# A long matmul pipeline on one core: transfers issued later, transposes on another queue, chunks entering one by one, another order of the last visits

## The chip, the cores and the metric

One core of a Trainium2 chip. The metric is the device time of one execution in microseconds (us), and lower is better. A run is marked slow when it is over 1.5% above the fastest run of the same kernel; only fast runs are compared unless the text says otherwise. PE is TensorE, DVE VectorE, ACT ScalarE, POOL GpSimd, SP SyncE. SP, ACT and POOL also issue DMAs, each from a queue of its own, in program order. A crossbar transpose is a DMA that transposes while it copies.

## The reference

A short causal convolution over the sequence, then a mixing layer with two 4224 x 4224 matrices:

```python
# x: (8, 4224, 192), weight: (8 heads, 7 taps)
w = softmax(weight)                                   # per head
out[b, s, h, g] = sum_k w[h, k] * x_pad[b, s + k, h, g]      # conv; its result is called x below
theta = x @ w_theta
zr, zi = x * cos(theta), x * sin(theta)
y = einsum('ts,bsd->btd', w_tok_r, zr) + einsum('ts,bsd->btd', w_tok_i, zi)
u = x + y
return u + maximum(u @ w_ch, 0)
```

The two big products are nearly all of the work. All inputs and the output are float32; the products run in bfloat16.

## The kernel before

The 4224 tokens are 33 chunks of 128 rows (source side) and 17 units of 256 rows (target side; the last has 128). A chunk is prepared once: conv on PE, copy out by ACT, transpose, theta on PE, sine and cosine on ACT, products and differences on DVE. It then stays in SBUF while 17 visits use it. A visit takes one unit and up to 11 resident chunks, multiplies, and adds the result to four partial sums of 128 x 768 float32, which live in DRAM between visits. A unit of 256 rows takes 7 products (of two halves each) per chunk instead of 8, so 14 matmuls of 384 columns.

```python
SLOTS = 11
FIRST = (0, 0, 1, 1, 2, 3, 3, 4, 5, 6, 7)      # visit in which each of the first chunks enters
# ... (cut)
    def conv(self, hp):
        ...
        if hp == H // 2 - 1:                       # the conv of the chunk is complete
            for a in range(NQ):                    # kept in DRAM as the residual of the end
                nc.sync.dma_start(out=xs[t0 : t0 + Q, :], in_=...)
# ... (cut)
    def transposed(u, by_pe, uT=None):
        if not by_pe:                              # from chunk 11 on, and for all outputs
            nc.sync.dma_start_transpose(out=uT[:, :, :], in_=u)
            return uT
# ... (cut)
class Visit:
    def load(self, q, tag):                        # one of six buffers for partial sums
        ...
        nc.sync.dma_start(out=d, in_=part[self.u][q][:, :])
        if self.final:                             # the last visit of a unit: add the residual
            nc.sync.dma_start(out=xr, in_=xs[self.rows(q), self.cols(q)])
            nc.gpsimd.tensor_tensor(out=d, in0=d, in1=xr, op=ALU.add)

    def add(self, q, y, g, begins=False, ends=False):
        ...                                        # DVE: d += y
        if self.final:
            self.output(q)                         # cast, transpose, u @ w_ch, relu, store
            return
        nc.sync.dma_start(out=part[self.u][q][:, :], in_=self.d[q])
        free_sums(self.tag[q])                     # issues the load of the next sum at once
```

The order of every engine is fixed when the program is built: a list of events (load, conv, transpose, theta, weights) is placed against the PE time that the program expects.

## Time and profile before

| | |
|---|---|
| time | 1751.27 us median of 4 runs (1741.36 to 1756.26) |
| span of the profiled run | 1748.8 us |
| PE busy / DVE / ACT / POOL | 85% / 61% / 19% / 40% |
| granted PE clock, mean | 0.92 |
| products of a visit of 11 chunks, undisturbed | 25.0 us |

"Busy in chosen stretches" has one row per stretch: its length, then for each engine the busy time and the number of instructions, the granted PE clock (1.00 is full), the busy share of the DMA engines (it can exceed 1) and the bytes moved in GB/s. A line of the waits says who waited, for whom, and the total, the number and the longest of the waits. The lines themselves are in the prediction.

### The profile page before, as it was taken

The numbers are of one execution on the slowest core, as the hardware profiler recorded it, in microseconds if no ns is written. First come the engines' busy times: TensorE is split into PE (matmuls) and PEld (weight loads), VectorE is DVE, ScalarE is ACT, GpSimd is POOL, SyncE is SP. The second block draws the span as 40 slices with busy tenths as digits, with TensorE's granted clock in tenths as the row PEclk, the third lists the DMA queues.
The fourth block names the chain that finished last, engine by engine and source line by source line (L and its number), as shares of the span: only waits on it lengthen the run. The fifth ranks groups of instructions, "written<-read, shape, count | busy, mean of one in ns | idle before, by whom it ended". The sixth has DMA issues, their size and how long they took to land. (4 is left out here: it accounts for less than half of the span.)

```text
span 1748.8 us, 25577 instructions
## 1 busy us (share of the span) xinstructions
PE 1487.3 (85%) x9390; PEld 904.5 (52%) x9390; DVE 1068.7 (61%) x1830; ACT 339.1 (19%) x582; POOL 703.2 (40%) x1176
## 2 busy tenths in 40 slices
PE   5779999999887878699999889899888878887543
PEld 3445666665554545466665555555555545554322
DVE  5778544543676767576657667668656636576533
ACT  4444212112221212110012112121111100111111
POOL 6654433332433334323333423423544435456621
PEclk7689999999998989899999999999999988998865
DMA  7898766665999999977889998999889868899865
GB/s 108 135 180 162 145 122 121 126 120 129 182 187 187 197 204 209 190 169 185 187 203 179 188 187 185 182 188 186 177 187 184 181 155 172 179 220 224 176 160 143
DMA packets 366861, 301.66 MB, mean 172 GB/s; under 512 B 174864, under 2 KB 316432, under 8 KB 366736
## 3 DMA queue, kind: packets, MB, share of 16 engines
q1 hardware_dynamic: 192464, 215.18, 44.5%
q0 software_dynamic: 174272, 84.86, 42.6%
q8 instruction: 73, 1.20, 0.3%
q14 instruction: 52, 0.43, 0.1%
HBM read 250.21 MB, written 106.56 MB: 204 GB/s over the span
## 5 line engine op out<-in xcount | busy, mean ns | idle before, releaser
L390 PEld LDWEIGHTS <-w 128*128 128x128 bf16 x6600 | 654.8, 100 | 467.6 <-issue 68.9
L313 POOL DMA_DIRECT2D st<-in_moe_w_tok_i_dram x476 | 257.0, 548 | 478.7 <-DVE w L333 428.6
L313 POOL DMA_DIRECT2D st<-in_moe_w_tok_r_dram x476 | 256.2, 546 | 284.6 <-DVE w L333 266.7
L405 DVE TENSOR_TENSOR d<-y,d 128x384 f32<-128x384 f32 x290 | 158.2, 552 | 238.0 <-PE y L390 188.0
L333 DVE STREAM_TRANSPOSE w<-st 128x768 bf16<-128x768 bf16 (+5 forms) x333 | 258.8, 813 | 60.6 <-PE x L390 59.8
L390 PE MATMUL x<-zi,w 128*128 128x384 bf16 x1122 | 218.9, 350 | 0.0
L390 PE MATMUL x<-zr,w 128*128 128x384 bf16 x1122 | 203.5, 332 | 0.0
L390 PE MATMUL s<-zt,w 128*128 128x384 bf16 x1056 | 188.4, 331 | 14.9 <-DVE d L405 14.9
L390 PE MATMUL y<-zr,w 128*128 128x384 bf16 x1056 | 189.8, 331 | 13.1 <-DVE d L405 13.1
L390 PE MATMUL y<-zt,wl 128*128 128x384 bf16 x1056 | 195.4, 339 | 5.5 <-DVE d L405 5.5
L390 PE MATMUL y<-zt,w 128*128 128x384 bf16 x1122 | 197.3, 329 | 1.5 <-ACT y L423 1.4
L287 PEld LDWEIGHTS <-uT 128*128 128x128 bf16 x792 | 82.1, 114 | 215.9 <-DMA uT<-xz 96.0
L377 POOL TENSOR_TENSOR d<-d,xr 128x768 f32<-128x768 f32 x66 | 109.7, 1663 | 193.8 <-DMA d<-part 157.8
L390 PE MATMUL s<-zi,w 128*128 128x384 bf16 x1056 | 185.8, 330 | 0.0
L287 PE MATMUL v<-wth,uT 128*128 128x192 bf16 x528 | 70.8, 287 | 105.6 <-DMA uT<-xz 87.8
L390 PEld LDWEIGHTS <-wl 128*128 128x128 bf16 x1056 | 105.9, 101 | 79.4 <-issue 15.9
L217 DVE TENSOR_SCALAR ang<-v 128x384 f32<-128x384 f32 x132 | 69.0, 551 | 122.7 <-PE v L287 120.1
L229 ACT ACTIVATE zr<-ang,half_pi 128x768 bf16<-128x768 f32 x66 | 60.6, 932 | 427.2 <-DVE ang L217 244.9
L348 DVE TENSOR_TENSOR w<-w 128x1408 bf16<-128x1408 bf16 (+10 forms) x174 | 134.2, 771 | 4.9 <-PE s L390 4.7
L405 DVE TENSOR_TENSOR d<-x,d 128x384 f32<-128x384 f32 x92 | 50.5, 554 | 120.3 <-PE x L390 78.5
L477 DVE SCALAR_TENSOR_TENSOR d<-v,d 128x384 f32<-128x384 f32 x132 | 68.0, 549 | 74.3 <-PE v L287 74.0
L405 DVE TENSOR_TENSOR d<-s,d 128x384 f32<-128x384 f32 x200 | 104.7, 536 | 14.2 <-PE s L390 10.5
(64 smaller groups left out, 876.4 us busy)
## 6 DMA issues: line engine op xcount, KB each, us to landing
part<-d SPq DMA_DIRECT2D x172, 384.0 KB, 3.7
d<-part SPq DMA_DIRECT2D x172, 384.0 KB, 4.3
out_dram<-d SPq DMA_DIRECT2D x66, 384.0 KB, 3.9
st<-in_moe_w_tok_r_dram POOLq DMA_DIRECT2D x260, 88.0 KB, 4.8
st<-in_moe_w_tok_i_dram POOLq DMA_DIRECT2D x260, 88.0 KB, 4.3
xs<-xz SPq DMA_DIRECT2D x132, 96.0 KB, 4.8
xr<-xs SPq DMA_DIRECT2D x66, 192.0 KB, 2.9
xw<-in_x_dram POOLq DMA_DIRECT2D x129, 96.0 KB, 5.4
```

The lines of the kernel that those rows point to most:

```text
L217: dve(nc.vector.tensor_scalar(out=af[:, k * 2 * D : (k + 1) * 2 * D], in0=channel_mix(self.xT[g], k, wth), scalar1=-CLAMP, scalar2=CLAMP, ...
L229: act(nc.scalar.activation(out=z[:, g * HN : (g + 1) * HN], in_=self.ang[g], func=AT.Sin, **({"bias": half_pi[:], "scale": 1.0} if i == 0 ...
L287: pe(nc.tensor.matmul(v[:, b * D : (b + 1) * D], lhsT=tT[:, 3 * k + b + i, :], rhs=w[:, 2 * b + i, :], start=(i == 0), stop=(i == 1),), D)
L313: nc.gpsimd.dma_start(out=st[a * Q : (a + 1) * Q, :, 0 : self.n * Q], in_=w[t * P : (t + 1) * P, t0 : t0 + self.n * Q].rearrange("(bt i) s ...
L333: dve(nc.vector.transpose(w[:, c:ce, :, :], st[:, :, c * Q : ce * Q].rearrange("p bt (c j) -> p c bt j", j=Q),))
L348: dve(nc.vector.tensor_tensor(out=flat(o), in0=flat(self.w[p]), in1=flat(self.w[q]), op=op))
L377: nc.gpsimd.tensor_tensor(out=d, in0=d, in1=xr, op=ALU.add)
L390: pe(nc.tensor.matmul(y[:, 0:PC], lhsT=weights[self.v].block(a, c), rhs=zs[c].operand(b, g), start=(start and c == self.lo), stop=(c == se ...
L405: dve(nc.vector.tensor_tensor(out=o, in0=y[:, 0:PC], in1=o, op=ALU.add))
L477: dve(nc.vector.scalar_tensor_tensor(out=dk, in0=channel_mix(uT, k, wch_[0]), scalar=0.0, in1=dk, op0=ALU.max, op1=ALU.add,))
```

## The change

Four intents: transfers go out only when their data is ready, so that a queue does not stand at them; the crossbar transposes move from SP's to ACT's queue; the first eleven chunks enter one per visit and are prepared within the visits; and the last visits alternate large and small, with four more sum buffers from the space of the chunk loads that have ended.

```diff
-    FIRST = (0, 0, 1, 1, 2, 3, 3, 4, 5, 6, 7)
+    FIRST = tuple(range(SLOTS))
@@ the order of the visits
+    while large:
+        sequence.append(large.pop(0))
+        if small:
+            sequence.append(small.pop())
@@ transposed
-            nc.sync.dma_start_transpose(out=uT[:, :, :], in_=u)
+            nc.scalar.dma_start_transpose(out=uT[:, :, :], in_=u)
@@ conv: the stores of the residual become keep(), called after the second transpose
@@ load of a sum
-                nc.sync.dma_start(out=xr, in_=xs[self.rows(q), self.cols(q)])
+                later(4.0, lambda: self.residual(q))     # issued on POOL, added 3 us later
@@ store of a sum (the store of an output likewise, 1.0 and 6.0)
-            nc.sync.dma_start(out=part[self.u][q][:, :], in_=self.d[q])
-            free_sums(self.tag[q])
+            def store():
+                nc.sync.dma_start(out=part[self.u][q][:, :], in_=self.d[q])
+                later(6.0, lambda: free_sums(self.tag[q]))
+            later(1.5, store)
@@ outputs: three in flight instead of four
@@ after the last conv
+        big = [wk.tile([P, 2, HN], F32, name="late", tag="xw") for _ in range(2)]
+        tags.extend(t[:, k, :] for t in big for k in range(2))
@@ load of a chunk two ahead instead of one
-            (-24.0, lambda: c + 1 < NCH and c + 1 > 2 and load_chunk(c + 1)),
+            (-15.0, lambda: c + 2 < NCH and load_chunk(c + 2)),
@@ early chunks: conv and transposes in visit c-2, theta and the rest in visit c-1
   ... (the rest cut)
```

More of the change, by code (lines that the diff above doesn't have):

```diff
@@ L119 @@
         visits.append((v % UNITS, here[0], here[-1] + 1))
+    settled = enter[-1]
+    large = [v for v in range(settled, len(visits))]
+    small = []
+    while len(large) > len(small) + 3:
+        small.append(large.pop())
+    sequence = list(range(settled))
+    while large:
+        sequence.append(large.pop(0))
+        if small:
+            sequence.append(small.pop())
     seen = [0] * UNITS
@@ L203, in conv, with keep @@
                 self.xf = self.xz[:, :, :].rearrange("p b d -> p (b d)")
-                for a in range(NQ):
-                    t0 = tokens(self.c, a)
-                    nc.sync.dma_start(
-                        out=xs[t0 : t0 + Q, :], in_=self.xf[a * Q : (a + 1) * Q, :]
-                    )
-                self.xT, self.ang = [], []
+                self.xT, self.ang = [], []
+        def keep(self):
+            for a in range(NQ):
+                t0 = tokens(self.c, a)
+                nc.sync.dma_start(
+                    out=xs[t0 : t0 + Q, :], in_=self.xf[a * Q : (a + 1) * Q, :]
+                )
         def transpose(self, g):
@@ L295, in __init__ @@
         def __init__(self, v):
-            self.u, self.lo, self.hi = visits[v]
+            self.u, self.lo, self.hi = visits[sequence[v]]
             self.n = self.hi - self.lo
@@ L364, in __init__ @@
             self.quarters = [3, 1, 0, 2] if self.pair else [1, 0]
-            self.d, self.tag = {}, {}
+            self.d, self.tag, self.missing = {}, {}, set()
         def load(self, q, tag):
-            pool, n = (dpool, 6) if tag == "sums" else (wk, 2)
-            d = pool.tile([P, HN], F32, name="d", tag=tag, bufs=n)
+            d = dpool.tile([P, HN], F32, name="d", tag="d") if tag is None else tag
             self.d[q], self.tag[q] = d, tag
@@ L374, in load, with residual, add @@
             if self.final:
-                xr = wk.tile([P, HN], BF16, name="xr", tag="xz")
-                nc.sync.dma_start(out=xr, in_=xs[self.rows(q), self.cols(q)])
+                self.missing.add(q)
+                later(4.0, lambda: self.residual(q))
+        def residual(self, q):
+            d = self.d[q]
+            xr = wk.tile([P, HN], BF16, name="xr", tag="xz")
+            nc.gpsimd.dma_start(out=xr, in_=xs[self.rows(q), self.cols(q)])
+            def add():
                 nc.gpsimd.tensor_tensor(out=d, in0=d, in1=xr, op=ALU.add)
+                self.missing.remove(q)
+            later(3.0, add)
         def rows(self, q):
@@ L390, in product @@
                 pe(nc.tensor.matmul(
-                    y[:, 0:PC], lhsT=weights[self.v].block(a, c),
+                    y[:, 0:PC], lhsT=self.w.block(a, c),
                     rhs=zs[c].operand(b, g),
@@ L398, in add @@
         def add(self, q, y, g, begins=False, ends=False):
-            while q not in self.d:
-                output_step()
+            while q not in self.d or q in self.missing:
+                if delayed:
+                    delayed.pop(0)[2]()
+                else:
+                    output_step()
             o = self.d[q][:, g * PC : (g + 1) * PC]
@@ L410, in add @@
                 return
-            nc.sync.dma_start(out=part[self.u][q][:, :], in_=self.d[q])
-            free_sums(self.tag[q])
+            def store():
+                nc.sync.dma_start(out=part[self.u][q][:, :], in_=self.d[q])
+                stored.add((self.u, q, self.hi))
+                later(6.0, lambda: free_sums(self.tag[q]))
+            later(1.5, store)
         def items(self):
             gs = range(NG)
+            self.w = weights[sequence.index(self.v)]
             x = [None] * NG
@@ L459, in output @@
         def output(self, q):
-            if len(outputs) == 4:
+            if len(outputs) == 3:
                 output_step()
-            made[0] += 1
-            if made[0] % 2:
-                ub = wk.tile([P, HN], BF16, name="ub", tag="ang")
-                uT = None
-            else:
-                both = wk.tile([P, 2, HN], BF16, name="ubT", tag="xw")
-                ub = both[:, 0, :]
-                uT = both[:, 1, :].rearrange("p (k s) -> p k s", s=P)
+            turn[0] += 1
+            if turn[0] % 3:
+                both = wk.tile([P, 2, HN], BF16, name="ubT", tag="ang")
+                ub, uT = both[:, 0, :], both[:, 1, :]
+            else:
+                ub, uT = (wk.tile([P, HN], BF16, name=n, tag="uT") for n in ("ub", "uT"))
+            uT = uT.rearrange("p (k s) -> p k s", s=P)
             act(nc.scalar.activation(out=ub, in_=self.d[q], func=AT.Copy))
-            outputs.append((clock[0] + 8.0, self, q, transposed(ub, False, uT)))
+            outputs.append((pos[0] + 8.0, self, q, transposed(ub, False, uT)))
         def output_end(self, q, uT):
@@ L481, in output_end, with store, later @@
             bs = slice(q % 2 * B // 2, (q % 2 + 1) * B // 2)
-            nc.sync.dma_start(
-                out=out[bs, self.rows(q), :].rearrange("b s d -> s b d"),
-                in_=d[:, :].rearrange("p (b d) -> p b d", d=D),
-            )
-            free_sums(self.tag[q])
+            def store():
+                nc.sync.dma_start(
+                    out=out[bs, self.rows(q), :].rearrange("b s d -> s b d"),
+                    in_=d[:, :].rearrange("p (b d) -> p b d", d=D),
+                )
+                later(6.0, lambda: free_sums(self.tag[q]))
+            later(1.0, store)
     wch_ = []
     outputs = []
-    made = [0]
-    tags = ["sums"] * 6
-    order = [Visit(v) for v in range(len(visits))]
+    delayed = []
+    stored = set()
+    pos = [0.0]
+    def later(us, fn):
+        delayed.append((pos[0] + us, len(made), fn))
+        made.append(None)
+        delayed.sort(key=lambda x: x[:2])
+    made = []
+    turn = [0]
+    tags = [None] * 6
+    order = [Visit(v) for v in sequence]
     waiting = [(vi, q) for vi in order for q in vi.quarters]
@@ L500, in load_sums @@
         while waiting and tags:
-            vi, q = waiting.pop(0)
+            vi, q = waiting[0]
+            if not (vi.first or (vi.u, q, vi.lo) in stored):
+                return
+            waiting.pop(0)
             vi.load(q, tags.pop(0))
@@ L579 @@
         weights[0].load()
-    load_chunk(2)
     def idle(n, s):
@@ L590, with length, last_conv @@
     cost = PC / 2400 + 0.0025
-    starts, t = [], 0.0
-    for u, lo, hi in visits:
-        starts.append(t)
+    starts, t = {}, 0.0
+    for v in sequence:
+        u, lo, hi = visits[v]
+        starts[v] = t
         t += (hi - lo) * parts(u) * cost
-    starts.append(t)
     events = []
+    def length(v):
+        u, lo, hi = visits[v]
+        return (hi - lo) * parts(u) * cost
+    def last_conv():
+        big = [wk.tile([P, 2, HN], F32, name="late", tag="xw") for _ in range(2)]
+        tags.extend(t[:, k, :] for t in big for k in range(2))
+        load_sums()
     def chunk_events(c, t0, n):
         for at, fn in (
-            (-24.0, lambda: c + 1 < NCH and c + 1 > 2 and load_chunk(c + 1)),
+            (-15.0, lambda: c + 2 < NCH and load_chunk(c + 2)),
             (-18.0, lambda: (chunks[c].conv(0), chunks[c].conv(1))),
-            (-15.0, lambda: (chunks[c].conv(2), chunks[c].conv(3))),
+            (-15.0, lambda: (
+                chunks[c].conv(2), chunks[c].conv(3), c == NCH - 1 and last_conv()
+            )),
             (-14.0, lambda: chunks[c].transpose(0)),
-            (-13.5, lambda: chunks[c].transpose(1)),
+            (-13.5, lambda: (chunks[c].transpose(1), chunks[c].keep())),
             (-5.0, lambda: chunks[c].theta(0)),
@@ L620, in chunk_events, with early, early_events @@
             events.append((t0 + 2 * n * cost + at, fn))
-    def early_events(c, t0):
-        for off, fn in (
-            (0.0, lambda: c + 1 < NCH and c + 1 > 2 and load_chunk(c + 1)),
-            (0.0, lambda: (chunks[c].conv(0), chunks[c].conv(1))),
-            (1.0, lambda: (chunks[c].conv(2), chunks[c].conv(3))),
-            (2.0, lambda: chunks[c].transpose(0)),
-            (3.0, lambda: chunks[c].transpose(1)),
-            (4.5, lambda: (chunks[c].theta(0), chunks[c].wave(0, 0), chunks[c].wave(1, 0))),
-            (6.0, lambda: (chunks[c].theta(1), chunks[c].wave(0, 1), chunks[c].wave(1, 1))),
-            (7.5, lambda: (chunks[c].times_x(0, 0), chunks[c].times_x(1, 0))),
-            (8.5, lambda: (chunks[c].times_x(0, 1), chunks[c].times_x(1, 1))),
-            (9.5, lambda: [chunks[c].sum(i) for i in range(4)]),
-        ):
-            events.append((t0 + off, fn))
-    EARLY_T = 30.0
+    def early(v):
+        return (starts[v], length(v)) if v >= 0 else (10.0 * v, 10.0)
+    def early_events(c):
+        for v, at, fn in (
+            (c - 2, 0.30, lambda: chunks[c].conv(0)),
+            (c - 2, 0.40, lambda: chunks[c].conv(1)),
+            (c - 2, 0.50, lambda: chunks[c].conv(2)),
+            (c - 2, 0.60, lambda: chunks[c].conv(3)),
+            (c - 2, 0.65, lambda: c + 2 < NCH and load_chunk(c + 2)),
+            (c - 2, 0.75, lambda: chunks[c].transpose(0)),
+            (c - 2, 0.85, lambda: (chunks[c].transpose(1), chunks[c].keep())),
+            (c - 1, 0.05, lambda: chunks[c].theta(0)),
+            (c - 1, 0.20, lambda: (chunks[c].wave(0, 0), chunks[c].wave(1, 0))),
+            (c - 1, 0.25, lambda: chunks[c].theta(1)),
+            (c - 1, 0.40, lambda: (chunks[c].wave(0, 1), chunks[c].wave(1, 1))),
+            (c - 1, 0.45, lambda: (chunks[c].times_x(0, 0), chunks[c].times_x(1, 0))),
+            (c - 1, 0.60, lambda: (chunks[c].times_x(0, 1), chunks[c].times_x(1, 1))),
+            (c - 1, 0.75, lambda: [chunks[c].sum(i) for i in range(4)]),
+        ):
+            t0, n = early(v)
+            events.append((t0 + at * n, fn))
     for c in range(NCH):
         if c < SLOTS:
-            early_events(c, -EARLY_T + c * 6.0)
+            early_events(c)
         else:
@@ L643 @@
             n = visits[v][2] - visits[v][1]
+            assert sequence[v] == v
             at = 10.05 if pair(visits[v][0]) else 4.05
@@ L663 @@
     for v in range(len(visits)):
-        t0, n = starts[v], starts[v + 1] - starts[v]
+        t0, n = starts[sequence[v]], length(sequence[v])
         if v == 0:
@@ L678 @@
     events.sort(key=lambda x: x[0])
-    pos = [-EARLY_T]
+    pos[0] = -30.0
     def run(until):
-        while outputs and outputs[0][0] <= clock[0]:
-            output_step()
-        while events and events[0][0] <= until:
-            events.pop(0)[1]()
+        while True:
+            at = [
+                (queue[0][0], i)
+                for i, queue in enumerate((outputs, delayed, events)) if queue
+            ]
+            if not at or min(at)[0] > until:
+                break
+            pos[0], i = min(at)
+            if i == 0:
+                output_step()
+            elif i == 1:
+                delayed.pop(0)[2]()
+            else:
+                events.pop(0)[1]()
+        pos[0] = until
     events.append((200.0, lambda: wch_.append(channel_weights(moe_w_ch, "wch"))))
@@ L697 @@
                 run(t)
-    while outputs:
-        output_step()
+    while outputs or delayed:
+        pos[0] += 1.0
+        run(pos[0])
 _INS = ['x', 'weight', 'moe_w_theta', 'moe_w_tok_r', 'moe_w_tok_i', 'moe_w_ch']
```

## The prediction

> **What bounds the kernel now.** I read the stages first (busy time in chosen stretches), then PE's waits, SP's waits, the DMA issues, and last the chain that ended last. TensorE (PE) is 85% busy, so the question is in which stretches it is not. I counted the 7656 product matmuls (384 columns each) along the trace to find where each of the 61 visits begins, and cut the span there:
>
> ```profile
> core 0: us, PE busy (x) PEld busy (x) DVE busy (x) ACT busy (x) POOL busy (x), PEclk, DMA share, GB/s
> 0.00:61.70 61.70, 35.46 (x231) 21.57 (x232) 38.09 (x90) 24.36 (x40) 40.84 (x86) 0.68 0.77 104
> 61.70:155.00 93.30, 75.67 (x526) 45.02 (x524) 73.83 (x148) 48.93 (x91) 47.38 (x87) 0.85 0.93 170
> 155.00:459.00 304.00, 304.00 (x1895) 183.25 (x1893) 150.99 (x214) 66.24 (x135) 110.28 (x206) 1.00 0.69 135
> 459.00:756.00 297.00, 241.44 (x1531) 145.15 (x1530) 198.24 (x359) 59.51 (x99) 109.19 (x200) 0.91 1.02 190
> 756.00:923.50 167.50, 167.50 (x1055) 101.03 (x1053) 108.34 (x167) 10.93 (x21) 56.92 (x106) 1.00 0.85 191
> 923.50:1244.90 321.40, 289.05 (x1854) 173.44 (x1853) 218.77 (x361) 59.35 (x100) 110.72 (x198) 0.95 0.98 184
> 1244.90:1592.00 347.10, 299.52 (x1909) 187.71 (x1907) 211.48 (x353) 47.45 (x66) 167.31 (x223) 0.94 0.90 185
> 1592.00:1748.80 156.80, 74.66 (x405) 47.30 (x402) 69.00 (x145) 22.32 (x32) 60.53 (x72) 0.72 0.72 171
> ```
>
> In the third and fifth rows PE never stops. There 310 product matmuls take 50 us, 0.1613 us each; I take that for full speed (half of it for a matmul of 192 columns). The whole program at full speed: 7656 x 0.1613 = 1235 us of products, 1584 matmuls of 192 columns (conv, theta, output mix) x 0.081 = 128, transposes on PE and warm-up 11: 1374 us. Of the 1749 us, 375 are lost. By stretch: 62 pass before the first product and 33 are lost in visits 0 to 3; 75 in visits 17 to 26 (459 to 756); 49 in 34 to 43; 61 in 44 to 54; 92 in 55 to 60; 20 after the last product.
>
> ```profile
> PE v L287 <- DMA uT<-xz: 87.8, 20, 7.3
> PE v L287 <- DMA uT<-ub: 46.7, 10, 6.7
> PE v L287 <- DVE d L477: 40.9, 7, 8.5
> ```
>
> PE's waits, longest in total first: it waits for the crossbar transpose of a chunk (uT<-xz) or of an output (uT<-ub), and at the very end for VectorE (DVE). Restricted to 459 to 756 the first wait is 55.6 us, all of PE's waits there; the other 20 us lost there are clock. Why is the transpose late? The queue that issues it, SP, is waiting for something else:
>
> ```profile
> SPq L411 <- DVE d L405: 325.7, 111, 8.2
> SPq L373 <- DMA part<-d: 264.3, 99, 6.8
> SPq L411 <- ACT d L403: 195.7, 29, 13.9
> SPq L376 <- POOL d L377: 140.0, 50, 6.8
> SPq L373 <- DMA out_dram<-d: 122.4, 49, 7.0
> ```
>
> SP, one queue in program order, waits over 1000 us: with a store for the last add, with a load for the store that frees its buffer. In the visit that begins at 550.8 the conv result is ready at 550.3, SP then stands 3 us at a load, and the transposes go out at 556.2 and 557.6; landing (8.5 us later) is 564.7, PE got there at 559.1. Median from issue to landing:
>
> ```profile
> uT<-xz SPq DMA_TRANSPOSE x44, 9.4
> uT<-ub SPq DMA_TRANSPOSE x33, 4.7
> ```
>
> The end, from the chain of waits, 1698 to 1709 (start, us, what):
>
> ```profile
> 1698.46 3.25 DMA d<-part
> 1701.86 0.09 issue
> 1701.95 1.64 POOL d L377
> 1703.62 0.57 DVE d L405
> ...
> 1705.95 3.43 DMA out_dram<-d
> 1709.40 3.12 DMA d<-part
> ```
>
> A sum buffer is loaded (3.2), gets its residual on POOL (1.6), is added, mixed, stored (3.4), and only then takes the next load: some 11 us a turn. The chain has seven such turns from 1650 to the end. Visits 55 to 60 hold 6, 5, 4, 3, 2, 1 chunks and each has four sums to pass through six buffers; they took 22, 25, 24, 23, 32, 31 us for 16 to 7 us of PE work.
>
> **What the Trainium skill says.** (1) "DMA: Bandwidth & Descriptors", section "Anatomy of one DMA": the DMA engines don't wait on semaphores, the issuing sequencer does before dispatch. The SP waits above agree: one unready store holds everything behind it. (2) Same page, "Issuing engines are not separate DMA queues": SP, ACT and POOL feed the same 16 engines. So another queue buys order, not bandwidth. (3) Same page, "Silent corruption": transposes issued from both SP and ACT could corrupt each other; here all move to ACT, so one stream remains. (4) "TensorE: Matmul & The Clock Gate", "The HAM clock gate": the clock goes to half when PE idles in a window of about 3.4 us. The trace agrees: after the 4.8 us wait that ends at 1038.6 the granted clock is 0.50 from 1038.8 to 1042.2, then 1.00. So a wait over some 3 us costs about 1.7 us more.
>
> **The change, part by part.**
>
> *Start.* A chunk now enters with each visit: visit v has v+1 chunks to visit 10, so only chunk 0 and the first weights are needed before the first product. In the instruction order, chunk 0's VectorE work is 14 instructions and the first weights 8. By before's trace: transposes copied at 16.7, first weights issued 11 to 20 on POOL and landed at about 23, second half of the wave about 26. First product: 27 us instead of 61.7. From there each visit carries one chunk's preparation; VectorE: 14 x 0.5 = 7 us, weights of the next visit 2.5 to 5, four adds 2.2: 11 to 15 us per visit against 5 to 14.5 of PE, for visits 0 to 4; together 65 us, visit 5 begins at 92. From visit 5 PE bounds: 16.8 + 19.0 + 21.3 + 22.2 + 23.9 + 24.8 = 128 at full speed, 8 more for waits: visit 11 begins at 228. Before it began at 316.5, but with 89 chunk-visits done against 66; 23 x 14 x 0.1613 = 52 us are put off to visits 17 to 26. Gain 316.5 - 52 - 228 = 36.
>
> *Visits 11 to 16:* unchanged, 142.5 us; ends at 371.
>
> *Visits 17 to 26.* Each now has 11 chunks instead of 8 to 10: the same weights are transposed and the same sums moved, in 10 visits of 27 us. Full speed 221 + 52 = 273. The transposes go out on ACT right after ACT's own copies (about 1 us after the conv); with 8.5 us to landing that is 9.5 to 10 us after the conv, and the program puts theta 10 us of products after it. Remaining wait 0 to 1 us per visit, below what halves the clock: 8 us in all. 281, ends at 652. Gain 75 - 8 = 67.
>
> *Visits 27 to 33:* 167.5 as before; 819.
>
> *Visits 34 to 43:* full speed 272, plus the same 8: 280, ends at 1099. Gain 41.
>
> *Last 17 visits.* Full speed 330. The order is now 11, 7, 11, 6, 11, 5, ... 11 (one row block, 8 parts), 1, 10, 9, 8 chunks. Ten buffers instead of six: four more come from the chunk buffers once the last conv is done. A buffer is held about 9 us from load to first use, 4 to 13 in use, 15 to the free: about 240 buffer-us per pair of visits, so a pair of 34 to 41 us needs 6 to 7 of ten; the turns should leave the critical path. VectorE takes their place in the small visits: 12 adds x 0.545 = 6.5, 8 output steps x 0.515 = 4.1, and the next large visit's weights (transposes 4 x (0.82 + 0.93) = 7.0, four sums 3.6): 21.2 us, against PE's 13.9, 11.6, 9.4 for 5, 4, 3 chunks. With some 4 us of slack from the PSUM banks I get 1 + 3.5 + 5.5 + 8 + 3 + 12 = 33 for chunks 6 to 1, 10 for half clock after these waits, 10 for outputs whose transpose is late. 383, ends at 1482; before 484 for the same products. Gain 101.
>
> *The end.* After the last product: cast, transpose, mix, store: about 13 us against 20. Span 1495.
>
> Sum of gains 36 + 67 + 41 + 101 + 7 = 252 (rounded) from 1749.
>
> *Added cost.* ACT issues 110 transposes, 1.2 to 1.8 us of its sequencer each. ACT's copies y<-x are needed about two products (7 us) later, so mostly hidden. The residual loads move from SP to POOL: 66 x 0.55 = 36 us on an engine 40% busy.
>
> **The rivals.**
> A. *DMA becomes the bound.* A visit of 34 to 43 moves 5.9 MB (185 GB/s x 32 us); in 27.4 us this is 217 GB/s, and the last part would need some 230. For: the share is already 0.98 to 1.02 there, and landing takes twice as long as in the quiet parts. Against: a slice at 224 GB/s exists, and the time of a packet includes its queueing. If it holds at 195 GB/s, visits take 30 us and the total is 1555 to 1580.
> B. *The transposes block ACT instead.* Its order is now serial with the buffer waits of the outputs, and y<-x sits behind q2's cast at each visit's end. For: the instruction order shows it so. Against: with 11 chunks y<-x has slack. Costs 2 to 4 us in each of 17 visits: 1530 to 1550.
> C. *The sums' turns remain the bound of the last visits,* because POOL in order stands at weight loads (it waits for VectorE 695 us) and the residuals sit behind them. Then only half of that gain comes: about 1545.
> D. *Better than thought:* VectorE falls behind less, transposes land in 5 us with their own ring: 1455.
>
> **Range and chances.** All parts reduce waits and no work is added, so slower would need a new wait of 250 us; I see none. Predicted 1495 us, 1450 to 1555 for 8 in 10. Faster by over 2%: 0.97, within 2%: 0.02, slower: 0.01.
>
> **What would show it.** First product near 27 us and visit 11 near 228; PE's wait for uT<-xz under 15 us in all and granted clock 0.98 or more from 371 to 1099; SP's waits with stores and loads far below 1000; no run of load, POOL, add, store in the chain at the end. In the last 390 us PE's waits are for VectorE's adds in small visits. Wrong: a DMA share over 1.1 with visits of 30 us (A), PE waiting for ACT (B), VectorE waiting for POOL (C).

## The result, and the profile after

The changed kernel takes 1548.64 us (median of 4 runs, 1542.33 to 1556.93). The ratio to the kernel before is 0.885, 95% interval 0.879 to 0.892. A ratio is the mean time of one kernel's fast runs over that of the other's of the same rounds, so not quite the ratio of the medians quoted. The profiled run is the slowest of the four, span 1555.2 us. In the second column of the next table, what the old entry of the chunks did early and the new one puts off, 52 us, is moved to visits 17 to 26. The control is the same code in a later job.

| stretch | before | predicted | after | control |
|---|---|---|---|---|
| to the first product | 61.7 | 27 | 28.0 | 28.6 |
| visits 0 to 10 | 203 | 201 | 205.3 | 204.4 |
| visits 11 to 16 | 142.4 | 142.5 | 142.4 | 142.4 |
| visits 17 to 26 | 349 | 281 | 285.9 | 279.8 |
| visits 27 to 33 | 167.4 | 167.5 | 167.4 | 167.4 |
| visits 34 to 43 | 321.5 | 280 | 289.6 | 290.3 |
| last 17 visits | 483.5 | 383 | 424.8 | 408.5 |
| end | 20.4 | 13 | 11.8 | 11.7 |
| span | 1748.8 | 1495 | 1555.2 | 1533.2 |

Busy time of the changed kernel in the stretches that the visits set (without visits 11 to 16 and 27 to 33):

```profile
core 0: us, PE busy (x) PEld busy (x) DVE busy (x) ACT busy (x) POOL busy (x), PEclk, DMA share, GB/s
0.00:28.00 28.00, 13.29 (x91) 7.22 (x91) 17.10 (x49) 9.73 (x16) 26.90 (x61) 0.87 0.82 93
28.00:233.30 205.30, 190.01 (x1339) 114.82 (x1338) 161.50 (x298) 95.41 (x185) 123.40 (x227) 0.98 0.98 185
...
375.70:661.60 285.90, 277.04 (x1854) 168.03 (x1853) 216.44 (x360) 59.35 (x100) 109.42 (x200) 0.99 1.10 208
...
829.00:1118.60 289.60, 277.40 (x1857) 168.24 (x1854) 217.18 (x359) 59.39 (x100) 112.50 (x201) 0.99 1.08 207
1118.60:1543.40 424.80, 354.35 (x2281) 221.70 (x2280) 288.31 (x490) 68.96 (x97) 264.93 (x359) 0.93 1.04 208
```

From 376 to 1119 the clock is 0.99 and PE idles only 9 to 12 us per ten visits. The last 17 visits are where time is still lost: 425 us for 330 us of work at full speed. PE's waits, whole run:

```profile
PE v L301 <- DMA uT<-xz: 21.0, 15, 4.4
PE v L301 <- DMA ubT<-ubT: 20.4, 10, 5.3
PE y L413 <- DVE d L431: 17.4, 3, 7.1
PE v L301 <- DMA uT<-ub: 15.9, 7, 6.4
```

The wait for a chunk's transpose fell from 87.8 to 21.0 us (14.9 in the control). The waits for an output's transpose (uT<-ub and ubT<-ubT are the same, in different buffers) are 36 us, against 51 before. Did the transposes become quicker? Here is their median from issue to landing:

```profile
uT<-xz ACTq DMA_TRANSPOSE x44, 9.3
ubT<-ubT ACTq DMA_TRANSPOSE x44, 5.7
```

They did not: 9.4 and 4.7 us before. What changed is when they go out. From the traces I measured, for the 22 chunks that use the crossbar, the time from the end of ACT's last copy to the issue of the first transpose: 4.4 us on average before, 0.0 after; to its landing, 13.1 us before and 8.2 after. For the 66 outputs it is less: from the end of the cast to the issue 2.5 us before and 0.0 after, but to the landing 7.0 before and 6.3 after. And SP's own waits:

```profile
SPq L386 <- DMA part<-d: 336.0, 108, 6.4
SPq L439 <- ACT d L429: 164.8, 18, 14.5
SPq L439 <- DVE d L431: 144.3, 69, 9.4
```

In all, SP waits 1228 us after and 1253 us before. SP still stands at unready transfers; only the transposes no longer stand behind it. From the end of the chain that ended last (start, us, what):

```profile
1440.36 15.15 DMA xr<-xs
...
1461.52 10.51 DMA st<-in_moe_w_tok_i_dram
...
1521.52 0.48 DVE d L431
1522.02 0.85 ACT ubT L501
1522.89 5.97 DMA ubT<-ubT
1528.91 0.83 PE v L301 x8
```

The loop of load, POOL, add and store that closed the chain before is gone. At the very end stand an add, a cast, the crossbar transpose and the mix. Earlier the chain runs through POOL's queue, which the change loaded more: a residual (xr) lands 15.15 us after its issue, POOL is idle for 12.3 us until it can add it, and weight loads (st) go out behind the add, one of which lands after 10.51 us. This falls in the visit of one chunk and the next one, which together lose 31 us of the 95 that the last 17 visits lose.

### The profile page after: what moved, and what is told of

The parts are those of the page before. It is cut to its first block, busy times and chain, and to the rows that moved or that the text cites. A ratio compares the mean times of both kernels' runs of the same rounds, so it can differ in the third digit from the quotient of the medians.

```text
span 1555.2 us, 25507 instructions
## 1 busy us (share of the span) xinstructions
PE 1425.6 (92%) x9390; PEld 869.5 (56%) x9390; DVE 1078.8 (69%) x1818; ACT 336.5 (22%) x582; POOL 743.7 (48%) x1242
## 4 chain that ended last, share of the span: by engine, by line
PE 61%; DMA 23%; DVE 5%; POOL 4%; issue 3%; ACT 3%; ACTq 1%; SPq 0%; DVEq 0%; POOLq 0%
PE y L413 25%; PE x L413 17%; PE s L413 14%; DMA uT<-xz 10%; PE v L301 3%; DMA ubT<-ubT 3%; DMA uT<-ub 2%; POOL st L327 2%; DMA xr<-xs 2%; DMA st<-in_moe_w_tok_i_dram 2%; PE pc L200 2%; DVE w L347 1%; DMA st<-in_moe_w_tok_r_dram 1%; ACTq L285 1%; DVE w L362 1%
## 5 line engine op out<-in xcount | busy, mean ns | idle before, releaser
L413 PEld LDWEIGHTS <-w 128*128 128x128 bf16 x6600 | 641.7, 98 | 449.2 <-issue 42.0
L347 DVE STREAM_TRANSPOSE w<-st 128x640 bf16<-128x640 bf16 (+4 forms) x324 | 258.2, 832 | 58.3 <-PE x L413 48.8
L431 DVE TENSOR_TENSOR d<-y,d 128x384 f32<-128x384 f32 x250 | 137.2, 553 | 179.3 <-PE y L413 165.5
L413 PE MATMUL x<-zi,w 128*128 128x384 bf16 x1122 | 199.0, 327 | 0.0
L455 ACT ACTIVATE y<-x 128x384 f32<-128x384 f32 x116 | 55.3, 478 | 221.3 <-PE x L413 209.3
L431 DVE TENSOR_TENSOR d<-s,d 128x384 f32<-128x384 f32 x174 | 91.1, 536 | 11.4 <-PE s L413 9.3
L397 POOL TENSOR_TENSOR d<-d,xr 128x768 f32<-128x768 f32 x38 | 62.7, 1654 | 74.1 <-DMA xr<-xs 34.0
L301 PEld LDWEIGHTS <-uT 128*128 128x128 bf16 x704 | 60.9, 100 | 64.0 <-DMA uT<-xz 27.9
L188 POOL DMA_DIRECT2D xw<-in_x_dram x132 | 76.8, 599 | 38.5 <-PE pc L200 34.8
L347 DVE STREAM_TRANSPOSE wl<-st 128x640 bf16<-128x640 bf16 (+5 forms) x104 | 81.2, 814 | 11.7 <-DMA st<-in_moe_w_tok_i_dram 11.7
```

The costliest lines, as they stand in the source:

```text
L188: nc.gpsimd.dma_start(out=self.xw[lo : lo + n, h, :, :], in_=x[:, t0 : t0 + n, :].rearrange("b s d -> s b d"),)
L301: pe(nc.tensor.matmul(v[:, b * D : (b + 1) * D], lhsT=tT[:, 3 * k + b + i, :], rhs=w[:, 2 * b + i, :], start=(i == 0), stop=(i == 1),), D)
L347: dve(nc.vector.transpose(w[:, c:ce, :, :], st[:, :, c * Q : ce * Q].rearrange("p bt (c j) -> p c bt j", j=Q),))
L413: pe(nc.tensor.matmul(y[:, 0:PC], lhsT=self.w.block(a, c), rhs=zs[c].operand(b, g), start=(start and c == self.lo), stop=(c == self.hi - 1 ...
L431: dve(nc.vector.tensor_tensor(out=o, in0=y[:, 0:PC], in1=o, op=ALU.add))
L455: act(nc.scalar.activation(out=y[g][:, 0:PC], in_=x[g][:, 0:PC], func=AT.Copy))
```

## The experiments

Twelve runs follow, all correct: eleven variants, and the changed kernel once more as the control. In the changed kernel's "last 17 visits", one profile of the same code differs from another by up to 16 us, in each of the other stretches by up to 10. Differences in us below are differences of ratios times the 1745 us of the kernel before. The reference for a ratio is 0.885 (first job) and 0.889 (control).

### Transposes back on SP

```diff
-            nc.scalar.dma_start_transpose(out=uT[:, :, :], in_=u)
+            nc.sync.dma_start_transpose(out=uT[:, :, :], in_=u)
```

> The changed kernel, with only the crossbar transposes put back on SP's queue. Theory (order in the queue): SP still waits over 1000 us in the changed kernel, with loads for the stores that free their buffers, so a transpose behind such a load is late again; PE's wait for transposes rises from 57 us to 130 or more, the clock halves after many of them, and the time is 1620 to 1660 us. Rival (issue only when ready is enough: SP's waits no longer stand where a transpose follows): PE's wait stays under 75 us and the time is within 15 us of 1549.

Measured: ratio 0.904 (0.899 to 0.910), 1583.48 us, so 33 us more by the first job's ratio, 27 by the control's: between the two theories, and below the first one's range. PE's wait for the chunks' transposes, and SP's timeline before one of them (start, us, line and what):

```profile
PE v L301 <- DMA uT<-xz: 43.5, 16, 5.6
```

```profile
503.48 2.08 SPq L386 DMA_DIRECT2D d<-part  x2
...
508.14 3.30 SPq L285 DMA_TRANSPOSE uT<-xz  x2
```

The transpose stands behind two loads of sums and four halo copies (2.4 us, the line left out): the queue does hold it back, by 2.9 us on average after ACT's copy instead of 0.0. That is less than the 4.4 of the kernel before, where the four stores of the residual and a load that waited stood ahead too (549 to 556 us of its trace). The loss lies in visits 17 to 43 (visits 17 to 26 lose 33 us instead of 13, 34 to 43 30 instead of 16); in the last 17 visits SP is no worse than ACT (417.8 us): there the outputs' transposes go out 1.4 us after the cast but land 4.8 us after their issue on average, against 0.0 and 6.3 on ACT.

### Only the transposes moved, in the kernel before

The same line, edited the other way in the kernel before.

> The kernel before with only the crossbar transposes moved to ScalarE's queue. Theory (they were late because SP stood at loads and stores ahead of them): PE's wait for uT<-xz falls from 88 us to under 40, the clock recovers with it, and 35 to 60 us go: 1690 to 1718. Rival (landing takes 9 us whoever issues, so little is gained without the other parts): above 1735.

Measured: ratio 0.954 (0.941 to 0.966) from two fast runs, 1652.43 and 1669.84 us; the other two, 1677.91 and 1678.89, count as slow. That is 69 us less by all runs and 81 by the fast ones, more than the theory's 35 to 60. The profile is of the run of 1678.89 us; its granted clock, 0.935, is that of the fast ones. It is 72 us shorter than before, and 67 of these lie in visits 17 to 26 and 34 to 43. The wait for uT<-xz fell from 88 to 20 us as expected, but 26.5 us of a new wait came with it: PE waits for y<-x, a product that ACT copies from one PSUM bank to another, and this copy now stands behind a transpose in ACT's queue. This kernel still issues the residual's stores and early loads as before, and the first transposes of the 22 chunks went out 1.4 us after the copy. The outputs' transposes land later on ACT: 6.1 us after the issue on average, against 4.5 in the kernel before, with nothing but the queue changed and nearly the same traffic (183 against 180 GB/s in the last 17 visits). The medians of those in the ubT tiles, here and in the changed kernel with the transposes back on SP:

```profile
ubT<-ubT ACTq DMA_TRANSPOSE x33, 6.2
```

```profile
ubT<-ubT SPq DMA_TRANSPOSE x44, 4.8
```

### The old order of the last visits

```diff
-    while large: ...                      # the alternation
+    sequence = list(range(len(visits)))
```

> The changed kernel with the last visits in their old order, large to small; the ten sum buffers stay. Theory (the alternation spreads the four sums of a visit over more time): visits 55 to 60 again wait for the turns of the buffers, though ten instead of six carry them, and lose 40 to 55 us; time 1570 to 1595. Rival (the buffers do it all, and the weights of a large visit prepared within a small one cost what the alternation saves): within 10 us of 1549.

Measured: ratio 0.882 (0.874 to 0.890), 1545.04 us. The rival was right: given ten buffers, the alternation is worth nothing that can be measured.

### Six sum buffers with the new order

```diff
-        tags.extend(t[:, k, :] for t in big for k in range(2))
-        load_sums()
+        return
```

> The changed kernel without the four additional sum buffers of the last visits; the alternation stays. Theory (a pair of visits needs 6 to 7 buffers, so six are short): the chain of load, residual, add, store comes back in the small visits, time 1565 to 1590. Rival (with the alternation six are enough): within 8 us of 1549.

Measured: ratio 0.892 (0.886 to 0.897), 1558.31 us: 11 us over the first job, 5 over the control, and the intervals overlap. Neither expectation was met cleanly. PE's waits for DVE's adds grew from 23 to 34 us, those for output transposes fell from 36 to 16, and the last 17 visits took 421.5 us, within the 408 to 425 of the changed kernel's two profiles.

### The old order and six buffers together

Both edits above.

> The changed kernel with the old order of the last visits and with six sum buffers: both halves of the tail's change taken away at once; the delayed issue and the residuals on POOL stay. Theory (either of the two suffices, which is why taking away one alone moved nothing): without both the turns of six buffers bound visits 55 to 60 again, which lose some 90 us as before; time 1595 to 1620. Rival (neither matters; the tail gained from the order of loads and stores in SP's queue): at most 1570.

Measured: ratio 0.908 (0.899 to 0.916), 1577.28 us, 33 to 39 us more than the changed kernel. PE's waits from visit 44 on:

```profile
PE y L410 <- DVE d L428: 33.9, 7, 8.6
PE v L298 <- DVE d L505: 22.6, 6, 5.9
```

PE waits for adds and mixes on sums whose buffers come late, as in the kernel before: from visit 44 on DVE waits 101 us for POOL's residual adds here and 80 us in the kernel before, but 1 us in the changed kernel, 8 with the old order alone and 36 with six buffers alone. So either half nearly suffices: alone each costs nothing or little time to leave out, and without both 33 to 39 us come back. 1577 us is less than the theory expected: the last six small visits lose 77 us here, against 92 in the kernel before. The two halves are thus not the whole gain in the tail.

### The old entry of the chunks

```diff
-    FIRST = tuple(range(SLOTS))
+    FIRST = (0, 0, 1, 1, 2, 3, 3, 4, 5, 6, 7)     # with the old early schedule and the old loads
```

> The changed kernel with the old entry of the first eleven chunks and their old schedule (first product after five chunks). Theory (the start is worth what the difference of the two starts shows, 31 us, and visits 17 to 26 lose no more than now with their shorter visits): time 1575 to 1590, first product near 60 us. Rival (visits 17 to 26 with 8 chunks instead of 11 crowd the transfers as in the kernel before, so the entry is worth more): 1600 or more.

Measured: ratio 0.915 (0.909 to 0.920), 1600.75 us, 46 to 52 us more. The rival's figure was met, by 0.75 us, though not its reason: visits 17 to 26 did not lose as much as in the kernel before (75 us). The edit also puts back the chunk loads of all visits, one ahead instead of two. The first product is at 61.0 us, and visit 11 begins 82 us later with 52 us more done: 30 of the loss are in the start. Visits 17 to 26, shorter, lose 22.5 us instead of 6.5 to 12.6, of it 11 in waits for ACT's copies. The last 17 visits were 9 us longer too, within what two profiles differ.

### Four outputs in flight

```diff
-            if len(outputs) == 3:
+            if len(outputs) == 4:
-            outputs.append((pos[0] + 8.0, self, q, transposed(ub, False, uT)))
+            outputs.append((pos[0] + 12.0, self, q, transposed(ub, False, uT)))
```

The fourth pair of tiles is in the buffers of xz, the residual's in those of uT.

> The changed kernel with four outputs in flight instead of three (the fourth pair of tiles in the buffers of xz, the residuals in those of uT) and 12 us instead of 8 from an output's cast to its mix. Theory (36 us of PE's waits in the last visits are for output transposes that land 6 us on average and up to 14 us after their issue): those waits fall under 12 us, the time to 1510 to 1528. Rival (VectorE's adds in the small visits and the sum buffers, held 4 us longer, take the place): 1540 or more.

Measured: ratio 0.889 (0.883 to 0.895), 1549.70 us. The rival's figure was met; by the ratios the time is that of the changed kernel. But the waits moved as the theory expected: for output transposes from 36 to under 10 us. Waits for DVE's mixes of outputs rose from 10 to 21 us, those for adds stayed near 23. So DVE took some 11 of the 27 us that the transposes gave up, and the rest is within the noise.

### Chunk loads away from the transposes

```diff
-            (-15.0, lambda: c + 2 < NCH and load_chunk(c + 2)),
+            (-4.0, lambda: c + 2 < NCH and load_chunk(c + 2)),
```

The stores of the residual move from -13.5 to -4.5 in the program as well.

> The changed kernel with the load of the chunk after next, its halo and the store of xz put some 10 us later, so that they no longer go out together with the transposes. Theory (the transposes of visits 16 to 43 land in 9 us because these transfers share the 16 DMA engines with them): landing falls to 5 to 7 us median, PE's wait for uT<-xz from 21 to under 8 us, time 1525 to 1538. Rival (the landing is set by weights and sums, or by the transpose itself): landing stays at 8 us or more and the time within 8 us of 1549.

Measured: ratio 0.892 (0.886 to 0.898), 1553.41 us; landing 9.7 us median, wait for uT<-xz 24.3 us. The theory's figures were not met, but the edit did not do what was meant. In the trace the chunk loads go out 12.8 us (median) after the first transpose instead of 2.8, and the halo copies 8.5 instead of 2.3, but the stores of the residual earlier, 2.7 instead of 7.3: SP did not keep to the planned places. Of the three kinds 214 transfers are in flight together with a pair of transposes, against 241 before. So what makes the transposes land late is left open: these transfers are not ruled out, nor are the weights and sums, which were not moved.

### The control

The changed kernel unedited, in the last job.

> The changed kernel once more, unedited, as the control on the chip of the next three. Every theory expects 0.885 of the kernel before, within 0.007; its stages also show how far one profile of the same code differs from another (5 to 10 us per stage by the runs so far).

Measured: ratio 0.889 (0.884 to 0.893), 1548.44 us (1534.91 to 1565.97, one of six slow).

### Every transfer at once

```diff
     def later(us, fn):
-        delayed.append((pos[0] + us, len(made), fn))
-        made.append(None)
-        delayed.sort(key=lambda x: x[:2])
+        fn()
```

> The changed kernel with every delayed transfer issued at once, in the place where the program makes it: stores right behind the last add, loads right behind the store that frees their buffer, residuals behind their load; the rest stays (transposes on ACT, entry of the chunks, order of the visits, ten buffers). Theory (issue when ready frees SP's queue, and is worth what the other parts leave unexplained): SP's waits grow from 1200 to over 1400 us and the time to 1580 to 1610. Rival (with the transposes gone from SP nothing urgent stands behind its waits): within 12 us of the control.

Measured: ratio 0.896 (0.890 to 0.901) against 0.889, 12 us more in the fast runs; over all six runs the means are 1569 and 1549, 20 us more. SP's waits are 1222 us, against 1200 in the control: the delays hardly shorten them. The theory's figures were not reached; by the fast runs the difference is at the rival's limit of 12 us. The last 17 visits of this kernel and of the control, then the same stretch of the version of the next run:

```profile
1111.30:1539.90 428.60, 354.79 (x2282) 222.64 (x2280) 288.35 (x490) 68.88 (x97) 267.50 (x362) 0.93 1.00 206
```

```profile
1113.00:1521.50 408.50, 353.71 (x2282) 221.90 (x2280) 288.45 (x490) 68.88 (x97) 264.05 (x358) 0.95 1.04 215
```

```profile
1112.60:1504.90 392.30, 348.95 (x2272) 221.25 (x2269) 283.80 (x488) 68.96 (x97) 262.69 (x358) 0.94 1.07 218
```

Up to visit 44 this kernel and the control agree within 2 us in every stretch, and the whole difference is in the last 17 visits. So with the transposes on ACT, delayed issue is worth nothing in the middle. At the end it may be worth some 12 us, which is not clearly shown: the intervals overlap, and the changed kernel's own first profile took 424.8 us there.

### Old order, ten buffers, four outputs in flight

The edits of the second and the fifth of the changed kernel's variants (old order, four outputs) together.

> The changed kernel with the old order of the last visits, ten sum buffers and four outputs in flight. Theory (late transposes cost some 20 us of the last visits and the alternation nothing): 10 to 25 us under the control. Rival (whatever is taken from the transposes comes back as waits for VectorE and the buffers): within 6 us of the control.

Measured: ratio 0.870 (0.866 to 0.874) from three fast runs (1515.65 to 1523.35 us), against 0.889. Three further runs took 1544 to 1556 and count as slow, so the mean of all six, 1535, is only 0.9% under the control's 1549; the gain is 1 to 2%. Up to visit 44 its profile is the control's; the last 17 visits take 392 us instead of 408. PE's waits for output transposes are 2.6 us. This version beats both kernels, by the fast runs and by all, though by all runs its lead over the control is within the scatter.

### One small visit elsewhere, four outputs in flight

```diff
+    sequence.remove(len(visits) - 1)
+    sequence.insert(sequence.index(len(visits) - 2) + 1, len(visits) - 1)
```

> The changed kernel with four outputs in flight, and with the visit of one chunk moved from before a visit of ten chunks to between the visit of two chunks and the one whose weights are only two blocks. Theory (in a small visit VectorE must make the weights of the next large one, 21 us of work against 5 to 12 us of PE): the 31 us lost in the visit of one chunk and the next one fall to under 15, time 15 to 35 us under the control. Rival (the sum buffers bound three small visits in a row): the loss only moves to these, within 8 us of the control.

Measured: ratio 0.884 (0.879 to 0.889), within 9 us of the control. The rival was right: the last 17 visits take 419 us, PE's waits for DVE's adds are 31 us, and the loss only moved. The visit of one chunk and the one after it lose 21.5 and 11 us again.

## Why the prediction was right or wrong

**The total: right, near the upper edge.** 1495 was predicted, in 1450 to 1555; the median is 1548.64.

**The start: right.** First product 27 predicted, 28.0 measured; visit 11 at 228, measured 233. The old entry, put back, confirms the term (36 predicted): 30 us in the start, and 46 to 52 in all. The prediction had charged visits 17 to 26 no extra loss for being short; they have some.

**Visits 17 to 43: right in mechanism, not in every detail.** 561 us predicted, 575 measured (570 in the control). A transpose after ACT's copy mostly lands in time; the remaining waits are 21 us, 15 in the control (the prediction has under 15). The step "9.5 to 10 us after the conv" holds for the first transpose (8.2 us from the copy), but the second one lands 11.0 us after its issue, not 8.5, and so takes all the room that it has. Twice, in visits 23 and 40, the wait was long enough to halve the clock (mean 0.95 over the visit); waits of some 2 us in visits 18, 19 and 21 left it at 1.00.

**The last 17 visits: the step that failed.** 383 predicted, 425 measured (408 in the control), so 53 us of loss predicted against 95 (78). By terms, without the end:

| term | predicted | measured | control |
|---|---|---|---|
| waits for DVE (adds and mixes) | 33 | 33 | 26 |
| waits for output transposes | 10 | 34 | 25 |
| half clock after waits | 10 | 24 | 24 |
| waits for ACT's copies | 0 | 4 | 3 |

The half clock is what the loss leaves beyond the waits. Two terms were mis-sized: "10 for outputs whose transpose is late", and with it "10 for half clock after these waits". The prediction gives no working for the first; the landing that it shows for outputs is that on SP's queue, 4.7 us median (mean 4.5, longest 6.9). On ACT's queue the mean is 6.3 us and the longest 14.0 (5.6 and 10.4 in the control), and 17 of the 66 outputs (9) land over the 8 us that the program leaves between cast and mix. It is the queue that goes with the longer landing, and not the heavier traffic: on SP the mean is 4.5 us at 180 GB/s and 4.8 at 209, on ACT 6.1 at 183 and 5.0 to 6.9 in the other versions, at 198 to 218. Why is open. With four outputs in flight, and 12 us from cast to mix, these waits fall under 10 us, so the room left for the transpose was too small; the time falls only where the old order stays (ratio 0.870), as in the alternation DVE takes part of it.

The forecast that PE's waits in this stretch are for VectorE's adds was wrong with it: they are 23 of 70 us.

**The reasons given for the tail were wrong in part.** The prediction gave the whole gain to the turns of the buffers leaving the path through alternation and ten buffers. Either one alone nearly does that; together they are worth 33 to 39 us of a gain of 67 in tail and end (504 to 437 us; 420 in the control, a gain of 84). Delayed issue accounts for some 12 us at most, which is not clearly shown. How much the residual's move to POOL's queue did was not tried.

**"SP's waits far below 1000" was wrong.** They are 1228 us. That forecast confused the queue's waiting with its harm: SP's waits cost what stands behind them. Of what was behind them, only the transposes were urgent.

**Rivals.** A (DMA the bound) did not come: visits of 34 to 43 take 29.0 us at 207 GB/s, not 30 at 195, though the DMA share of 1.08 and the chunks' landing, still some 9 us, belong to it. B (ACT blocked) is 3.8 us here, but 26 in the kernel with only the transposes moved. C (buffers still the bound) no: from visit 44 on VectorE waits 1 us for POOL, though POOL stands at residual loads for 48 us. D (transposes land in 5 us with their own ring) no: on ACT the chunks' transposes land 9.3 us after the issue (8.7 in the control), on SP 8.2 (medians), and the outputs' land later on ACT. The Trainium skill's sentence that all queues feed the same 16 engines ("DMA: Bandwidth & Descriptors", "Issuing engines are not separate DMA queues") agrees with the chunks' landing; the difference for the outputs it does not explain.

**Small misreadings in the prediction.** In the visit that begins at 550.8 the copy of the conv result ended at 549.84 (550.31 is SP's first store of it), and SP stood 2.4 us at the load, not 3. The last of the small visits has some 4 us of PE work, not 7. None of this moves the sum.

**Open.** What makes transposes land up to 15 us after their issue; why the second is later than the first by some 3 us on ACT and by only 0.5 on SP; why the outputs' transposes land later on ACT; and which of residual stores after the transposes, loads two chunks ahead and longer visits halved the loss of visits 17 to 26 (76 to 33 us) with the transposes still on SP.

## What to carry to other kernels

Before asking whether a queue waits, ask what urgent transfer stands behind the wait: moving one such transfer to another queue, right after the instruction that makes its data, was worth 27 to 33 us here and 69 to 81 in the kernel before, where more stood ahead of it, although it lands no sooner after its issue. Take landing times for a forecast from the queue that will issue the transfer (6.1 us on ACT and 4.5 on SP for the same transposes), and look at the longest of them, not only the median. Read in the trace whether an edit moved what it was to move. And leave out two remedies of the same wait both singly and together, since each alone may look worthless while the other covers it.

## What the Trainium skill lacked or had wrong

- "DMA: Bandwidth & Descriptors", "Issuing engines are not separate DMA queues", says that issuing from several engines saves only the issue time on the sequencer, which is usually small. It leaves out the waits of the transfers ahead on the same sequencer: the first transpose left 4.4 us after its data was ready on SP, 0.0 on ACT; moving the transposes alone took 69 to 81 us of 1740.
- No page has a difference in landing between SP's queue and ACT's: the same output transposes landed 4.5 us after the issue on SP and 6.1 on ACT, on average.
- "DMA: Bandwidth & Descriptors", "DMA Transpose (X-bar)", has no time for a transpose within SBUF; the bandwidths that the skill gives for transposes elsewhere are not said to be beside other traffic. Of 128 x 768 bfloat16 the issue took 1.2 to 4.8 us of the sequencer, the landing 2.7 to 15.3 us. In one stretch with two such transposes, a chunk load and weights, the changed kernel moved 140 GB/s at a share of 1.27, against 207 over visits 34 to 43:

```profile
1004.00:1020.00 16.00, 11.58 (x68) 7.09 (x67) 8.09 (x13) 0.02 (x1) 6.28 (x12) 0.91 1.27 140
```
